# Rows of the second batch scaled in place, and their low halves subtracted on GpSimd

## The chip, the cores and the metric

The kernel runs on one core of a Trainium2 chip. The metric is the device time of one execution in microseconds (us): the median of three runs. A core has five engines with a queue of their own each, and each works through its queue in order: TensorE (PE, with its weight loads as PEld), VectorE (DVE), ScalarE (ACT), GpSimd (POOL), and SyncE (SP), which here only issues transfers.

## What is computed

Three layers one after the other, on 2304 rows (4 batches of 576) of 512 columns:

```python
def phi(x):                                   # q and k scaled by D**-0.25, D = 64
    proj = np.einsum('bhsd,md->bhsm', x, omega)
    sq = np.sum(x * x, axis=-1, keepdims=True) / 2.0
    h = proj - sq
    h = h - np.max(h, axis=-1, keepdims=True)
    return np.exp(h) / np.sqrt(m)
...
kv, z = np.einsum('bhsm,bhsd->bhmd', k_p, v), np.sum(k_p, axis=2)
num = np.einsum('bhsm,bhmd->bhsd', q_p, kv)
den = np.einsum('bhsm,bhm->bhs', q_p, z)[..., None] + 1e-06
attn = num / den                              # (4, 8, 576, 64), then rows of 512
h = attn @ w_in                               # 512 -> 2048
x = (h * (1 / (1 + np.exp(-1.702 * h)))) @ w_out
out = ((x @ w_a) * (x @ w_b)) @ w_out2        # 512 -> 1536 -> 512
```

## The kernel before, in words

Attention goes batch by batch, and in a batch by pairs of heads (hp 0 to 3), first k, then q. A pair is one tile `raw` of 128 partitions by T = 9 row groups by D = 64 columns, 576 columns in float32, loaded by SyncE. `features` makes the exponential features of a tile. For the first batch (`nm[1] == "0"`) TensorE does this in float32. For the others each number is split into a pair of float16 numbers, high and low half, in the tile `x16` (tag A, two buffers): line 402 writes the high half on ScalarE, scaled by S_QK = 32, line 403 the low half on VectorE, as the scaled row minus the high half. A transposing transfer (line 408, issued by SyncE) brings the pairs into `xt` (tag B, two buffers), and TensorE multiplies them with omega's two halves (lines 414 and 415). Beside that come the squares of the rows. For the second batch (SQACC = "1") ScalarE does them in nine pieces of 64 columns with an accumulating output (line 422), four before and five after the next load is issued; they overwrite the raw tile. Then row maxima (line 480, VectorE), the exponent's offset (line 486), the exponentials (line 446, ScalarE).

From the second batch on, attention is interleaved with the feed-forward layer of the batch before (`ffn1`): products `ph` (lines 654 to 656), a tanh (line 662, ScalarE), a product with it (line 665, VectorE), a float16 pair (lines 671 and 672), products `y` (lines 685 to 687). While the first batch's feed-forward layer runs, the weights `w_in` and `w_out` are loaded 1 MB at a time into two buffers and turned into float16 pairs: three passes on VectorE that put the float64 bits together as float32 (lines 214, 254 and 262), the high half on ScalarE (line 272), the low half on VectorE (line 221).

The order of each engine's instructions is made by a scheduler when the program is built, from the order of the code and from which buffers are free. An instruction that stands early in a queue and waits holds all that stands behind it. TensorE's filler products (line 1110, `idle`) stand between the first batch's last steps.

Of the kernel before, what the change touches and what calls it, by code (L numbers as in the profile page):

```python
# [12 lines left out]
AF = mybir.ActivationFunctionType  # L13
ALU = mybir.AluOpType
# [6 lines left out]
S_QK = 2.0**5  # L21
# [12 lines left out]
def fused_kernel(  # L34
# [13 lines left out]
    nc = tc.nc  # L48
# [17 lines left out]
    SQROOT = (0.5 / float(D) ** 0.5) ** 0.5  # L66
# [305 lines left out]
    def features(pool, nm, x, e16, e32, psp, extra, shift=0):  # L372
# [26 lines left out]
                nc.tensor.matmul(pvs[2][:, 0, :], xm[D:, :], om_f[D:], start=True, stop=True)  # L399
        else:  # L400
            x16 = pool.tile([P, T, 2, D], F16, tag="A", name=f"x16_{nm}")
            nc.scalar.activation(out=x16[:, :, 0, :], in_=x, func=AF.Copy, scale=S_QK)
            nc.vector.scalar_tensor_tensor(
                out=x16[:, :, 1, :], in0=x, scalar=S_QK, in1=x16[:, :, 0, :],
                op0=ALU.mult, op1=ALU.subtract,
            )
            xt = pool.tile([P, T, P], F16, tag="B", name=f"xt_{nm}")
            own["xt", nm] = nc.sync.dma_start_transpose(
                out=xt, in_=x16.rearrange("p t j d -> p (t j d)")
# [7 lines left out]
        groups, pairs = (GROUPS_F, PAIRS_F) if nm[1] == "0" else (GROUPS, PAIRS)  # L417
        sq = pool.tile([P, T], F32, tag="sq", name=f"sq_{nm}")

        def squares(lo, hi):  # L420
            for t in range(lo, hi):
                nc.scalar.activation(
                    out=x[:, t], in_=x[:, t], func=AF.Square, scale=SQROOT, accum_out=sq[:, t : t + 1]
                )

        if nm[1] in SQACC:
            yield
            squares(0, NT)
        else:
            nc.scalar.activation(out=x, in_=x, func=AF.Square, scale=SQROOT)  # L430
            yield
            nc.vector.tensor_reduce(out=sq, in_=x, axis=AX.X, op=ALU.add)
        extra()
        yield
        if nm[1] in SQACC:
            squares(NT, T)
# [27 lines left out]
        for gi in range(len(GROUPS) + 2):  # L464
# [4 lines left out]
            if 1 <= gi <= len(GROUPS):  # L469
# [4 lines left out]
                if pair[0] not in mxs:  # L474
# [6 lines left out]
                    out=mx[:, ms], in_=pv[:, : len(g), :], axis=AX.X, op=ALU.max  # L481
                )
                if gi - 1 == pair[-1]:

                    for o, i0, scale in ((mh, mx, PROJ), (nb, mh, -1.0)):
                        own["nb"] = nc.vector.scalar_tensor_tensor(
                            out=o[:, : z - a], in0=i0[:, : z - a], scalar=scale, in1=sq[:, a:z],
                            op0=ALU.mult, op1=ALU.subtract,
# [19 lines left out]
    def kphase32(pool, b, hp, psp, nxt, f32=True):  # L508
# [4 lines left out]
        if not f32:  # L513
# [20 lines left out]
            return  # L534
        e32 = pool.tile([P, T, M], F32, tag="e16", name=f"e32_{nm}")
        yield from features(pool, nm, raw, None, e32, psp, nxt)
        pk = psp()[:, 0 : 2 * VC].rearrange("p (h c) -> p h c", h=2)
        nc.tensor.matmul(pk, e32[:, 2 * NT, :], vm, start=True, stop=False)
# [8 lines left out]
    def qphase(pool, b, hp, xT, psp, nxt, f32=False):  # L547
# [5 lines left out]
        if f32:  # L553
            e32 = pool.tile([P, T, M], F32, tag="e16", name=f"e32_{nm}")
            yield from features(pool, nm, raw, None, e32, psp, nxt)
            eq = pool.tile([P, T * P], F32, tag="eqT", name=f"eT32_{nm}")
            eT = eq.rearrange("p (t m) -> p t m", m=P)
# [694 lines left out]
```

## Time and profile before

| | before |
|---|---|
| runs, us | 900.38, 901.43, 902.91 |
| median, us | 901.43 |
| the profiled execution, us | 899.4 |
| its span, first to last instruction, us | 897.6 |
| TensorE, VectorE, ScalarE, GpSimd busy, us | 872.3, 690.9, 455.3, 1.4 |
| 55 to 140 us: TensorE, VectorE, ScalarE busy, us | 81.81, 80.34, 61.58 |
| TensorE's granted clock in both stretches read below | 1.00 of full speed |

The profile is one execution. Its durations are of single instructions; where instructions of an engine overlap a little, the time from one start to the next is what counts. The second batch's attention lies between about 55 and 140 us; its first k tiles are begun some 20 us earlier, beside the first batch's last steps.

### The profile page before, as it was taken

How to read it: one execution, taken by the hardware profiler on the slowest of the kernel's cores; microseconds unless marked ns; L12 is line 12 of the kernel's file. 1: busy time of each engine (PE TensorE's matmuls, PEld its weight loads, DVE VectorE, ACT ScalarE, POOL GpSimd, SP SyncE). 2: the span in 40 equal slices, each digit the busy share in tenths (PEclk: the TensorE clock that was granted, in tenths of full speed). 3: DMA queues.
4: the chain of work that ended last, by engine and by line, in shares of the span. 5: the costliest groups of instructions: out<-in, count | busy, mean ns of one | idle time of the engine just before them, and what ended most of it. 6: DMA issues, size and time to landing. Idle time of an engine off the chain costs nothing.

```text
span 897.6 us, 17390 instructions
## 1 busy us (share of the span) xinstructions
PE 872.3 (97%) x7094; PEld 626.3 (70%) x7094; DVE 690.9 (77%) x1244; ACT 455.3 (51%) x1087; POOL 1.4 (0%) x10
## 2 busy tenths in 40 slices
PE   8999999999999999999999999999999999999997
PEld 6864555644554455444448888888888888888886
DVE  5889999778797787999923399777999558566766
ACT  7777774677566776454323354544443122233221
POOL 0000000000000000000000000000000000000000
PEclk9999999999999999999999999999999999999999
DMA  7856895453674323885401055212332022223312
GB/s 205 242 142 162 205 228 197 120 120 82 137 161 110 75 40 67 146 259 222 135 7 49 24 177 175 106 43 83 134 126 83 5 40 84 83 99 125 87 39 71
DMA packets 129343, 105.35 MB, mean 117 GB/s; under 512 B 97776, under 2 KB 111088, under 8 KB 127216
## 3 DMA queue, kind: packets, MB, share of 16 engines
q1 hardware_dynamic: 128558, 103.66, 41.2%
q8 instruction: 55, 0.90, 0.4%
q10 hardware_dynamic: 706, 0.59, 0.2%
q14 instruction: 24, 0.20, 0.1%
HBM read 71.07 MB, written 17.69 MB: 99 GB/s over the span
## 4 chain that ended last, share of the span: by engine, by line
PE 59%; DVE 21%; DMA 7%; ACT 7%; issue 2%; ACTq 0%; SPq 0%; DVEq 0%
PE ph L655 3%; PE ph L654 3%; PE ph L656 3%; PE y L685 3%; PE y L686 3%; PE y L687 3%; DMA xt_k<-x_k 3%; PE oA L904 2%; PE oA L902 2%; PE oA L903 2%; PE pbA L811 2%; PE pbA L809 2%; PE pbA L810 2%; PE paA L809 2%; PE pa L568 2%
## 5 line engine op out<-in xcount | busy, mean ns | idle before, releaser
L686 PE MATMUL y<-gl,w_out 128*128 128x512 f16 (+1 forms) x320 | 114.4, 358 | 0.9 <-DVE gl L672 0.8
L687 PE MATMUL y<-gh,w_out 128*128 128x512 f16 (+1 forms) x320 | 114.2, 358 | 0.0
L685 PE MATMUL y<-gh,w_out 128*128 128x512 f16 (+1 forms) x320 | 111.9, 358 | 0.8 <-ACT gh L671 0.7
L654 PE MATMUL ph<-xT,w_in 128*128 128x512 f16 x256 | 97.1, 379 | 1.5 <-DMA xT<-x_q_3x 0.7
L655 PE MATMUL ph<-xT,w_in 128*128 128x512 f16 x256 | 97.1, 379 | 0.3 <-DVE xT L623 0.3
L656 PE MATMUL ph<-xT,w_in 128*128 128x512 f16 x256 | 97.1, 379 | 0.0
L665 DVE SCALAR_TENSOR_TENSOR th<-th,ph 128x512 f32<-128x512 f32 (+1 forms) x80 | 50.3, 629 | 39.9 <-ACT th L662 39.7
L662 ACT ACTIVATE th<-ph 128x512 f32<-128x512 f32 (+1 forms) x80 | 44.2, 553 | 48.8 <-PE ph L656 48.8
L671 ACT ACTIVATE gh<-th 128x512 f16<-128x512 f32 (+1 forms) x80 | 47.1, 588 | 42.0 <-DVE th L665 41.9
L672 DVE SCALAR_TENSOR_TENSOR gl<-th,gh 128x512 f16<-128x512 f32 (+1 forms) x80 | 50.7, 634 | 15.9 <-ACT gh L671 15.5
L809 PE MATMUL paA<-forms,w_a 128*128 128x256 f16 (+1 forms) x240 | 61.0, 262 | 1.6 <-DVE ca L828 0.8
L809 PE MATMUL pbA<-forms,w_b 128*128 128x256 f16 (+1 forms) x240 | 61.1, 262 | 0.9 <-DVE cb L828 0.9
L811 PE MATMUL pbA<-forms,w_b 128*128 128x256 f16 (+1 forms) x240 | 61.0, 262 | 0.0
L811 PE MATMUL paA<-forms,w_a 128*128 128x256 f16 (+1 forms) x240 | 61.0, 262 | 0.0
L810 PE MATMUL pbA<-forms,w_b 128*128 128x256 f16 (+1 forms) x240 | 61.0, 262 | 0.0
L810 PE MATMUL paA<-forms,w_a 128*128 128x256 f16 (+1 forms) x240 | 61.0, 262 | 0.0
L902 PE MATMUL oA<-w_o,ab 128*128 128x256 f16 x216 | 58.9, 273 | 1.6 <-ACT ab L860 0.9
L904 PE MATMUL oA<-w_o,ab 128*128 128x256 f16 x216 | 58.9, 273 | 0.6 <-DVE ab L861 0.5
L903 PE MATMUL oA<-w_o,ab 128*128 128x256 f16 x216 | 58.9, 273 | 0.0
L817 ACT COPY ka<-paA 128x512 f32<-128x512 f32 (+1 forms) x30 | 16.3, 543 | 78.2 <-PE paA L811 78.1
L910 DVE SCALAR_TENSOR_TENSOR o<-oA,o 128x512 f32<-128x512 f32 (+1 forms) x45 | 28.5, 633 | 34.2 <-PE oA L904 34.2
L687 PEld LDWEIGHTS <-w_out 128*128 128x128 f16 x320 | 31.4, 98 | 29.9 <-issue 3.0
(209 smaller groups left out, 2353.5 us busy)
## 6 DMA issues: line engine op xcount, KB each, us to landing
wraw<-in_moe_w_out_dram SPq DMA_DIRECT2D x14, 1024.0 KB
forms<-fd SPq DMA_DIRECT2D x8, 1792.0 KB
wraw<-in_moe_w_in_dram SPq DMA_DIRECT2D x8, 1024.0 KB
fd<-forms SPq DMA_DIRECT2D x4, 1792.0 KB
wraw<-in_moe_w_a_dram SPq DMA_DIRECT2D x6, 1024.0 KB
wraw<-in_moe_w_b_dram SPq DMA_DIRECT2D x6, 1024.0 KB
vt<-in_v_dram SPq DMA_DIRECT2D x16, 256.0 KB
rawq<-in_q_dram SPq DMA_DIRECT2D x16, 256.0 KB
```

Of the source, the lines that this page charges most:

```text
L654: nc.tensor.matmul(ph[:, :n], w[:, 0, c, fs], xh(c), start=(c == 0), stop=False)
L655: nc.tensor.matmul(ph[:, :n], w[:, 0, c, fs], xl(c), start=False, stop=False)
L656: nc.tensor.matmul(ph[:, :n], w[:, 1, c, fs], xh(c), start=False, stop=(c == KC - 1))
L685: nc.tensor.matmul(o, w[:, 0, f % 4, cs], gh[f][:, :n], start=(f == 0), stop=False)
L686: nc.tensor.matmul(o, w[:, 0, f % 4, cs], gl[f][:, :n], start=False, stop=False)
L687: nc.tensor.matmul(o, w[:, 1, f % 4, cs], gh[f][:, :n], start=False, stop=(f == FC1 - 1))
L809: nc.tensor.matmul(o[:, i], wh, xh, start=first, stop=False, skip_group_check=True)
L810: nc.tensor.matmul(o[:, i], wh, xl, start=False, stop=False, skip_group_check=True)
L811: nc.tensor.matmul(o[:, i], wl, xh, start=False, stop=final, skip_group_check=True)
L902: nc.tensor.matmul(bank[:, t], lh, wh, start=first, stop=False, skip_group_check=True)
L903: nc.tensor.matmul(bank[:, t], lh, wl, start=False, stop=False, skip_group_check=True)
L904: nc.tensor.matmul(bank[:, t], ll, wh, start=False, stop=final, skip_group_check=True)
```

## The change

For the second batch alone, ScalarE first scales the raw tile in place (float32), then copies it to the high half; the low half is a plain difference of the two on GpSimd. The squares read the scaled rows, so their factor is divided by S_QK. All other batches stay as they were.

```diff
             x16 = pool.tile([P, T, 2, D], F16, tag="A", name=f"x16_{nm}")
-            nc.scalar.activation(out=x16[:, :, 0, :], in_=x, func=AF.Copy, scale=S_QK)
-            nc.vector.scalar_tensor_tensor(
-                out=x16[:, :, 1, :], in0=x, scalar=S_QK, in1=x16[:, :, 0, :],
-                op0=ALU.mult, op1=ALU.subtract,
-            )
+            if nm[1] == "1":
+                nc.scalar.activation(out=x, in_=x, func=AF.Copy, scale=S_QK)
+                nc.scalar.copy(x16[:, :, 0, :], x)
+                nc.gpsimd.tensor_tensor(
+                    out=x16[:, :, 1, :], in0=x, in1=x16[:, :, 0, :], op=ALU.subtract
+                )
+            else:
+                nc.scalar.activation(out=x16[:, :, 0, :], in_=x, func=AF.Copy, scale=S_QK)
+                nc.vector.scalar_tensor_tensor(
+                    out=x16[:, :, 1, :], in0=x, scalar=S_QK, in1=x16[:, :, 0, :],
+                    op0=ALU.mult, op1=ALU.subtract,
+                )
...
+        root = SQROOT / S_QK if nm[1] == "1" else SQROOT
...
-                    out=x[:, t], in_=x[:, t], func=AF.Square, scale=SQROOT, accum_out=sq[:, t : t + 1]
+                    out=x[:, t], in_=x[:, t], func=AF.Square, scale=root, accum_out=sq[:, t : t + 1]
```

The scheduler builds another order from it on all engines, in the second batch and, to a lesser degree, in the third. Lines behind the edit are 7 to 9 numbers higher in the changed kernel. In the rows below the names are the tiles written and read: `rawk_0_814` and `rawk_1_817` are the second batch's k tiles, `rawq_0_1102` (after: 1106) and so on its q tiles, `x_k_0` a tile of pairs, `eT_q_0` the first batch's transposed features.

ScalarE, at the end of the first batch's attention. Before:

```order
L446 ACTIVATE e_q_0_311<-pa,nb_q_0_1_425 128x128 x8
L544 COPY kv_128<-pa 128x130 [waits PE_49]
L430 ACTIVATE rawq_3_456<-rawq_3_456 128x576 [waits DMAHW6_49,DMAHW5_49,PE_49]
L402 ACTIVATE x_k_0_856<-rawk_0_814 128x9x64 [waits DMAHW2_49,DMAHW1_49,PE_49]
L563 COPY eT_q_0_514<-pa 128x512 [waits PE_49]
```

ScalarE, the same place in the changed kernel:

```order
L455 ACTIVATE e_q_0_311<-pa,nb_q_0_1_425 128x128 x8
L403 ACTIVATE rawk_1_817<-rawk_1_817 128x576 [waits DMAHW4_49,DMAHW3_49]
L553 COPY kv_128<-pa 128x130 [waits PE_49]
L403 ACTIVATE rawq_0_1106<-rawq_0_1106 128x576 [waits DMAHW6_49,DMAHW5_49]
L439 ACTIVATE rawq_3_456<-rawq_3_456 128x576 [waits PE_49]
L403 ACTIVATE rawq_1_1214<-rawq_1_1214 128x576 [waits DMAHW7_49,DMAHW0_49]
L403 ACTIVATE rawq_2_1329<-rawq_2_1329 128x576 [waits DMAHW2_49,DMAHW1_49,Activation_49]
L404 CAST x_k_0_856<-rawk_0_814 128x9x64 [waits PE_49,Activation_49]
L572 COPY eT_q_0_514<-pa 128x512 [waits PE_49]
```

Four in-place passes stand here that were not there (a fifth, of `rawk_0_814`, stands four rows above), those of the q tiles behind waits for their loads; the copy `eT_q_0` stands behind all of them.

ScalarE, around the first tanh of the feed-forward layer (`th_0`). Before:

```order
L622 CAST xT_100<-pa 128x512 [waits PE_49]
L272 ACTIVATE w_in_87<-wf_841 128x4x256 [waits DVE_49]
L662 ACTIVATE th_0_914<-ph_0_844 128x512 [waits PE_49]
L422 ACTIVATE rawk_1_817,sq_k_1_910<-rawk_1_817 128x64 [waits DVE_49]
L422 ACTIVATE rawk_1_817,sq_k_1_910<-rawk_1_817 128x64 x3
L662 ACTIVATE th_1_939<-ph_1_862 128x512 [waits PE_49]
```

ScalarE, the same place in the changed kernel:

```order
L631 CAST xT_100<-pa 128x512 [waits PE_49]
L431 ACTIVATE rawk_1_817,sq_k_1_912<-rawk_1_817 128x64
L404 CAST x_k_2_974<-rawk_2_820 128x9x64 [waits DMAHW5_49,Activation_49]
L403 ACTIVATE rawk_3_823<-rawk_3_823 128x576 [waits DMAHW1_49,DMAHW0_49]
L403 ACTIVATE rawq_3_1444<-rawq_3_1444 128x576 [waits DMAHW7_49]
L404 CAST x_k_3_1065<-rawk_3_823 128x9x64 [waits DMAHW2_49,Activation_49]
L272 ACTIVATE w_out_89<-wf_882 128x1024 [waits DVE_49]
L671 ACTIVATE th_0_916<-ph_0_844 128x512 [waits PE_49]
L671 ACTIVATE th_1_941<-ph_1_863 128x512 [waits PE_49]
```

The casts of the third and fourth k tiles and two in-place passes now stand ahead of the first tanh. The cast of the fourth waits (DMAHW2) for the transposing transfer of the second, whose buffer of pairs it takes.

## Rows read from the trace of the kernel before

**Rows 1.** The page: busy us of each engine (share of the span), number of instructions.

```profile
PE 872.3 (97%) x7094; PEld 626.3 (70%) x7094; DVE 690.9 (77%) x1244; ACT 455.3 (51%) x1087; POOL 1.4 (0%) x10
```

**Rows 2.** Busy time in two stretches; stretch, its length, engines, granted clock, DMA share, GB/s.

```profile
55.00:140.00 85.00, 81.81 (x509) 45.12 (x507) 80.34 (x134) 61.58 (x239) 0.00 (x0) 1.00 0.76 201
28.00:55.00 27.00, 26.93 (x236) 24.04 (x235) 22.85 (x56) 22.33 (x76) 0.00 (x0) 1.00 0.72 187
```

**Rows 3.** Waits of TensorE, 55 to 160 us: total us, times, longest.

```profile
PE pa L414 <- ACT e_k L446: 1.7, 1, 1.7
PE pa L414 <- ACT e_q L446: 0.7, 1, 0.7
PE ph L654 <- DVE th L665: 0.4, 1, 0.4
PE ph L655 <- DVE xT L623: 0.3, 1, 0.3
```

**Rows 4.** Groups on VectorE, 55 to 140 us: busy us, mean ns | idle before, releaser.

```profile
L254 DVE SCALAR_TENSOR_TENSOR wf<-wraw,wf 128x1024 int32<-128x1024 int32 x11 | 13.4, 1221 | 0.0
L262 DVE SCALAR_TENSOR_TENSOR wf<-wraw,wf 128x1024 int32<-128x1024 int32 x11 | 13.4, 1218 | 0.0
...
L672 DVE SCALAR_TENSOR_TENSOR gl<-th,gh 128x512 f16<-128x512 f32 x12 | 8.1, 685 | 0.0
...
L221 DVE SCALAR_TENSOR_TENSOR w_in<-wf,w_in 128x1024 f16<-128x1024 f32 x6 | 7.3, 1218 | 0.3 <-ACT w_in L272 0.3
L221 DVE SCALAR_TENSOR_TENSOR w_out<-wf,w_out 128x1024 f16<-128x1024 f32 x6 | 7.3, 1212 | 0.0
...
L403 DVE SCALAR_TENSOR_TENSOR x_q<-rawq,x_q 128x576 f16<-128x576 f32 x4 | 3.0, 754 | 1.3 <-ACT x_q L402 1.3
L403 DVE SCALAR_TENSOR_TENSOR x_k<-rawk,x_k 128x576 f16<-128x576 f32 x3 | 2.2, 749 | 0.0
```

**Rows 5.** Chain of waits, 59 to 90 us: start us, us, what.

```profile
62.80 0.67 DVE x_k L403
...
72.81 3.23 DMA xt_k<-x_k
...
76.12 0.68 ACT x_q L402
...
78.82 0.22 PE pa L414
...
83.25 6.76 DMA xt_k<-x_k
```

**Rows 6.** ScalarE in order of time, 27.9 to 35.6 us: start, us, [idle before, releaser].

```profile
27.95 0.37 ACT L446 ACTIVATE e_q<-pa,nb_q 128x128 f32<-128x128 f32 x1 [0.60 <-DVE nb_q L486]
...
31.91 0.27 ACT L544 COPY kv<-pa 128x130 f32<-128x130 f32 x1 [0.81 <-PE pa L540]
32.47 0.68 ACT L430 ACTIVATE rawq<-rawq 128x576 f32<-128x576 f32 x1 [0.28 <-PE pa L384]
33.78 0.68 ACT L402 ACTIVATE x_k<-rawk 128x576 f16<-128x576 f32 x1 [0.63 <-PE pa L399]
34.37 0.58 ACT L563 COPY eT_q<-pa 128x512 f32<-128x512 f32 x1
...
35.37 0.27 ACT L563 COPY eT_q<-pa 128x128 f32<-128x128 f32 x1
```

**Rows 7.** TensorE in order of time: product reading eT_q, first feed-forward product.

```profile
36.45 1.33 PE L568 MATMUL pa<-kv,eT_q 128*128 128x65 f32 x10
...
54.63 0.38 PE L654 MATMUL ph<-xT,w_in 128*128 128x512 f16 x1
```

**Rows 8.** Groups on GpSimd, whole span: its longest instruction.

```profile
L313 POOL MEMSET vm<- 128x520 f32 x1 | 0.5, 531 | 0.0
```

**Rows 9.** ScalarE in order of time, 60 to 64 us.

```profile
61.64 0.60 ACT L662 ACTIVATE th<-ph 128x512 f32<-128x512 f32 x1 [1.48 <-PE ph L656]
63.50 0.26 ACT L422 ACTIVATE rawk<-rawk 128x64 f32<-128x64 f32 x1 [1.26 <-DVE x_k L403]
```

## The prediction, made before the changed kernel ran

> **What bounds the kernel now.** I read the busy shares first, then the stretch that the change touches, then its waits and its chain. TensorE is busy for 97% of the span and GpSimd for 1.4 us [rows 1]; over the whole program nothing but TensorE's own work is long enough to set the time. The second batch's attention runs in one stretch, from about 55 to 140 us, under the first batch's feed-forward tile, and there the page's average misleads. In those 85 us TensorE is busy for 81.81, VectorE for 80.34 and ScalarE for 61.58 [rows 2]. So two engines are close to full there, and VectorE is the one that the change relieves. In the stretch ahead of it (28 to 55 us, the first batch's last steps) TensorE is busy for 26.93 of 27 us, partly with filler products, and ScalarE for 22.33 [rows 2].
>
> What TensorE waits for in the stretch is little: the four waits of [rows 3] sum to 3.1 us, and two smaller ones of 0.2 us each are left out there. Two name VectorE (0.4 and 0.3 us), two name ScalarE's exponentials (1.7 and 0.7 us). The chain says how they came about. Shortly before the 0.4 us wait, VectorE itself stands on the chain, with one of this change's subtractions (0.67 us) [rows 5]. Before the 1.7 us wait a transposing transfer holds ScalarE, which waits for it in front of its scaling of a q tile and only then comes to the exponentials that TensorE needs [rows 5]. These waits are all that the change can win here: 3.1 us, or 3.5 with the small ones, of some 900.
>
> **What it takes off VectorE.** Eight subtractions at line 403 go, one for each pair of heads of k and q in the second batch. Each takes about 0.75 us by itself and 0.67 us of VectorE's time from its start to the next one's [rows 4, 5]. Seven lie in the stretch (four for q, three for k [rows 4]), one before it: 7 x 0.67 = 4.7 us. VectorE also stands idle for 1.3 us ahead of two of the q ones, because they wait for ScalarE [rows 4]; that goes too. Together 6.0 of VectorE's 85 us.
>
> **What it adds to ScalarE.** Eight more passes over 576 columns. One scaled pass of that size takes 0.68 us, and 0.59 us from its start (33.78) to the next start (34.37) [rows 6]: 8 x 0.59 = 4.7 us in all. ScalarE is 73% busy in the stretch, so what matters is where they stand. The in-place pass needs only the loaded rows and no free buffer of float16 pairs, so five of the eight move ahead, into the end of the first batch, in front of the copy eT_q that starts at 34.37. ScalarE has idle pieces there of 0.60, 0.81, 0.28 and 0.63 us [rows 6]. Two passes fit into the first two. Three do not fit wholly: 3 x 0.59 - 0.28 - 0.63 = 0.86 us late. The product that reads eT_q starts at 36.45 [rows 7], while its last copy starts at 35.37 and takes 0.27 [rows 6], so it has 36.45 - 35.64 = 0.81 us to spare. What is left is about 0.1 us. One unknown remains: ScalarE waits in order for the third q tile's load. If that lands late, the exponentials, eT_q and a weight conversion queued behind it wait as well. The trace does not show its landing, so I bound it: nothing, or 1 us. I take 0.2 us for this place, nearer to nothing because the loads were issued several microseconds earlier.
>
> The other place is the end of the first batch's rows, about 55 to 64 us. There the squares of the second k tile now wait for GpSimd, and the last copy into xT stands behind them on ScalarE; four passes and the casts of two k tiles stand ahead of the first tanh. ScalarE idles 1.48 and 1.26 us between 60 and 64 us [rows 9], which covers four passes of 0.59 us (2.4 us). What the waits add on top I put between 0 and 2 us, and take 0.5.
>
> **What it gives GpSimd.** Eight subtractions of 576 columns with two operands read from SBUF. GpSimd has no such row in the trace. The nearest is a fill of 520 columns, 0.53 us [rows 8], or 0.59 us for 576 columns. That is the lower end; three such passes, one for each operand and one for the result, are 1.8 us, the upper end. I take two passes, 1.2 us. Its own duration is mostly hidden. The transposing transfers that wait for it are also paced by TensorE giving back their target buffers. What is not hidden is whether GpSimd and VectorE can read SBUF at once. If they can, nothing is added. If GpSimd keeps VectorE out for as long as it runs, seven pieces of 1.2 us (8.4 us) come on top, more than the 6.0 that went. No row shows it, since GpSimd never worked beside VectorE here. I take the middle, 4.2 us, as one of the two ends alone would need a reason.
>
> What VectorE does there makes this the main question: 13.4 + 13.4 + 7.3 + 7.3 + 8.1 = 49.5 of its 80.3 us are instructions with two operands in SBUF, without those that go [rows 4]. On this the Trainium skill speaks against the change: in SBUF — State Buffer, section Who interferes with whom, it says that a VectorE instruction with two SBUF inputs and a GpSimd instruction that reads SBUF exclude each other, and that the one that comes second stands still until the first is through. By that rule this term is the whole 8.4 us and not 4.2, and the time comes out as the second rival below; no run here shows it yet. The price of the subtraction by the GPSIMD Engine Reference, section Performance versus the Vector engine (2.6 cycles for an element at 1.2 GHz), is an estimate of 1.25 us, which would leave the sum as it is.
>
> **The sum.** VectorE: -4.7 - 1.3 + 4.2 = -1.8 us in the stretch. The two waits of TensorE that name VectorE hold 0.7 us [rows 3], and TensorE is nearly full beside it, so I let 0.3 us of it arrive at the end. With the two places on ScalarE: +0.2 + 0.5 - 0.3 = +0.4 us. The profiled execution took 899.4 us (897.6 us span and 1.8 us around it), the median of the three runs is 901.43, so +2.0 us over the profile; I put the change on the median: 901.43 + 0.4 = 901.8 us.
>
> **The rivals.**
> *No interference (faster).* GpSimd and VectorE run side by side, all 6.0 us are won, and the six waits of TensorE (3.1 + 0.4 = 3.5 us) close nearly all: -3.3 us, with +0.2 at the start: 898.3 us. For it: VectorE stands directly before a wait of TensorE in the chain [rows 5], and earlier subtractions let the k transfers go earlier. Against it: the largest wait hangs on a transfer and on ScalarE's order [rows 5], and ScalarE gets more to do.
>
> *GpSimd holds VectorE up (slower).* Each GpSimd subtraction that lies in the stretch stops VectorE. VectorE was busy for 80.34 us and idle for 4.66, 1.3 of which goes [rows 2, 4]. It needs 80.34 - 4.7 + 3.36 = 79.0 us without GpSimd's pieces; with seven of 1.2 us 87.4, with seven of 1.8 us 91.6, against 85. Converted weights, tanh products and row maxima then come 2.4 to 6.6 us later, and TensorE, which has only some 3 us of idle time, waits for them. With 1.5 us each it is +4.5, and +0.7 from ScalarE: 906.6 us (904.5 to 908.7). It decides from 6.0 / 7 = 0.86 us of standstill for each subtraction. For it: two thirds of VectorE's time there are two-operand instructions. It is the case in which the change does not do what it says: the work would leave VectorE and its time would not. It is also the case of the Trainium skill's rule on the shared port named above.
>
> *ScalarE's order (slower, a little).* The cast of the fourth k tile now stands ahead of the first tanh and waits until the second k tile's transfer has freed a buffer. In this kernel one such transfer took 3.23 us to release ScalarE, a later one 6.76 [rows 5]. If the one in question is of the second kind, that is 3.5 us more; the squares and casts that stand between cover a part, and I let 2.0 us reach the tanh and the products behind it: 901.4 + 0.7 + 2.0 = 904.1 us.
>
> **How the numbers follow.** I give the forecast 0.45, no interference 0.20, the hold-up 0.25, ScalarE's order 0.10. The predicted time is 901.8 us. From 898.0 to 907.0 it holds the forecast (900.5 to 903.5), the fast case, ScalarE's order and two thirds of the hold-up: about 0.85. A measurement tells some 0.3%, or 2.7 us, from no change, so faster means under 898.7 and slower over 904.1. Faster: most of the first rival, 0.18. Slower: nearly all of the hold-up, half of ScalarE's order and a tail of the forecast, 0.32. The same: 0.50.
>
> **What would show it.** In the changed kernel's profile: GpSimd's eight subtractions and their length (0.6 to 1.8 us, 1.2 by my price); VectorE's two-operand instructions in 55 to 140 us, whose mean of 1.22 us for 1024 columns stays as it is where nothing holds them and grows, or whose starts spread, where GpSimd does; the start of the first feed-forward product, 54.63 now [rows 7], which I expect at most 0.5 us later; TensorE's waits in 55 to 160 us, 3.5 us now, which I expect between 2.5 and 4.5. I am wrong if the start moves by more than 1 us, if VectorE loses more than 6 us to GpSimd, or if a wait for GpSimd itself stands on the chain.

## The result, and the profile after

The changed kernel takes 905.97 us, the median of 7 runs from 904.74 to 912.2, beside 902.79 for the kernel before (7 runs, 900.38 to 903.83). The ratio is 1.0055, with a 95% interval of 1.0028 to 1.0081. Measured again beside the experiments below it was 1.0100 (1.0072 to 1.0128). By the two ratios the change costs 5 and 9 us (2.5 to 11.5 with the intervals). Two executions near 1510 us, at a granted clock of about 0.55, are left out of every median and ratio below. The profiled execution took 904.89 us, its span 903.0, and 5.4 us more than the span before.

First the busy line of the page after, to set beside [rows 1].

```profile
PE 872.0 (97%) x7094; PEld 627.0 (69%) x7094; DVE 693.7 (77%) x1236; ACT 459.7 (51%) x1095; POOL 16.1 (2%) x18
```

VectorE lost eight instructions (1244 to 1236) and is busy for 2.8 us longer. The two stretches of [rows 2], after (stretch, length, busy time of each engine, granted clock, DMA share, GB/s):

```profile
28.00:55.00 27.00, 25.53 (x224) 22.64 (x222) 23.18 (x51) 23.71 (x74) 2.16 (x1) 1.00 0.73 190
55.00:140.00 85.00, 78.85 (x499) 44.69 (x498) 82.53 (x127) 65.08 (x249) 12.56 (x7) 1.00 0.71 196
```

TensorE is busy for 1.40 us less in the first and 2.96 us less in the second. From 200 to 300 us it is 1.1 us less (97.46 before, 96.38 after), in code that the change doesn't touch. These three make the 5.4 us of the span, nearly. VectorE in the second stretch has 4.7 us of subtractions less and is busy for 2.2 us more: 80.34 before, 82.53 after.

TensorE's waits from 55 to 160 us, as [rows 3] (total us, times, longest):

```profile
PE pa L421 <- ACT e_k L455: 2.3, 3, 1.2
PE ph L663 <- DVE th L674: 2.2, 1, 2.2
PE ph L664 <- DVE xT L632: 1.2, 1, 1.2
PE pa L421 <- ACT e_q L455: 0.3, 1, 0.3
```

Together 6.0 us in place of 3.5. The wait for th went from 0.4 to 2.2, the one for xT from 0.3 to 1.2.

**Where GpSimd meets VectorE.** GpSimd's subtractions in two groups (busy us, mean ns), and then three of the eight in order of time (start, us):

```profile
L405 POOL TENSOR_TENSOR x_k<-rawk,x_k 128x576 f16<-128x576 f32 x4 | 7.7, 1914 | 57.3 <-DVE mx_q L489 34.3 <-ACT x_k L404 23.0
L405 POOL TENSOR_TENSOR x_q<-rawq,x_q 128x576 f16<-128x576 f32 x4 | 7.1, 1765 | 42.6 <-ACT x_q L404 42.6
```

```profile
56.62 2.32 POOL L405 TENSOR_TENSOR x_k<-rawk,x_k 128x576 f16<-128x576 f32 x1 [18.12 <-ACT x_k L404]
...
76.97 2.22 POOL L405 TENSOR_TENSOR x_q<-rawq,x_q 128x576 f16<-128x576 f32 x1 [10.00 <-ACT x_q L404]
...
103.75 1.28 POOL L405 TENSOR_TENSOR x_q<-rawq,x_q 128x576 f16<-128x576 f32 x1 [11.14 <-ACT x_q L404]
```

And VectorE beside them:

```profile
57.71 1.37 DVE L638 TENSOR_TENSOR x16r<-xf_q,x16r 64x128 f16<-64x128 f32 x1
...
76.70 0.16 DVE L495 SCALAR_TENSOR_TENSOR mh_k<-mx_k,sq_k 128x5 f32<-128x5 f32 x1
76.83 1.23 DVE L254 SCALAR_TENSOR_TENSOR wf<-wraw,wf 128x1024 int32<-128x1024 int32 x1
77.97 1.24 DVE L495 SCALAR_TENSOR_TENSOR nb_k<-mh_k,sq_k 128x5 f32<-128x5 f32 x1
...
103.33 0.68 DVE L489 TENSOR_REDUCE mx_k<-pa 128x4 f32<-128x512 f32 x1
103.94 2.17 DVE L254 SCALAR_TENSOR_TENSOR wf<-wraw,wf 128x1024 int32<-128x1024 int32 x1
```

Read them together. At 76.97 GpSimd starts while VectorE is inside a two-operand instruction (line 254, until 78.06). It comes through only behind that and ends at 79.19: 2.22 us. VectorE's next two-operand instruction, five columns that take 0.16 us elsewhere, starts at 77.97 and ends at 79.21. At 103.75 VectorE reads PSUM (line 489); GpSimd runs at once, and 1.28 us is its own length. VectorE's next instruction (line 254) takes 2.17 in place of 1.22. Seven instructions in the stretch (one of them line 214, with one operand) are lengthened so, by 1.09, 0.47, 0.45, 1.08, 0.96, 0.95 and 1.08 us: 6.1 us.

One of them can be followed to TensorE. The five columns at 77.97 are the offset that the exponentials e_k need, and ScalarE stands for them:

```profile
79.24 0.26 ACT L431 ACTIVATE rawk<-rawk 128x64 f32<-128x64 f32 x1 [1.39 <-DVE nb_k L495]
```

It comes to e_k at 80.22, and TensorE, which waits for e_k, stands 1.18 us until 81.38. By these rows 1.08 us of it are GpSimd's hold-up.

**Where the start moved.** ScalarE in order of time ([rows 6] before), and TensorE's first product behind the copy eT_q:

```profile
33.32 0.74 ACT L403 ACTIVATE rawq<-rawq 128x576 f32<-128x576 f32 x1
34.95 0.68 ACT L403 ACTIVATE rawq<-rawq 128x576 f32<-128x576 f32 x1 [0.89 <-DMA rawq<-in_q_dram]
...
36.10 0.58 ACT L572 COPY eT_q<-pa 128x512 f32<-128x512 f32 x1
```

```profile
36.73 0.33 PE L570 MATMUL pa<-ident,e_q 128*128 128x128 f32 x1 [1.29 <-ACT eT_q L572]
```

ScalarE waits 0.89 us for the third q tile's load, and the copy eT_q starts at 36.10 and not at 34.37. The one that waits for it is not the product of [rows 7] but a transposition (line 570) that needs the PSUM buffer which eT_q empties. The first feed-forward product starts at 56.23 and not at 54.63.

### The profile page after: what moved, and what is told of

The parts are those of the page before. It is cut to its first block, busy times and chain, and to the rows that moved or that the text cites. A ratio compares the mean times of both kernels' runs of the same rounds, so it can differ in the third digit from the quotient of the medians.

```text
span 903.0 us, 17404 instructions
## 1 busy us (share of the span) xinstructions
PE 872.0 (97%) x7094; PEld 627.0 (69%) x7094; DVE 693.7 (77%) x1236; ACT 459.7 (51%) x1095; POOL 16.1 (2%) x18
## 4 chain that ended last, share of the span: by engine, by line
PE 58%; DVE 24%; ACT 7%; DMA 7%; issue 3%; SPq 0%; ACTq 0%; DVEq 0%
PE y L694 3%; PE ph L663 3%; PE ph L664 3%; PE y L695 3%; PE ph L665 3%; PE y L696 3%; PE oA L913 2%; PE oA L911 2%; PE oA L912 2%; PE pa L577 2%; PE pbA L818 2%; PE pbA L820 2%; PE pbA L819 2%; DVE wf L254 2%; PE paA L818 2%
## 5 line engine op out<-in xcount | busy, mean ns | idle before, releaser
L826 ACT COPY ka<-paA 128x512 f32<-128x512 f32 (+1 forms) x30 | 16.3, 544 | 78.2 <-PE paA L820 78.1
L664 PEld LDWEIGHTS <-w_in 128*128 128x128 f16 x320 | 31.4, 98 | 30.8 <-issue 3.9
```

The costliest lines, as they stand in the source:

```text
L664: nc.tensor.matmul(ph[:, :n], w[:, 0, c, fs], xl(c), start=False, stop=False)
```

## The experiments

Each is given as a ratio to the kernel before on the same chip, with its interval. The first group takes the change apart.

| kernel | median us (before) | ratio, 95% interval |
|---|---|---|
| changed, first | 905.97 (902.79) | 1.0055 (1.0028 to 1.0081) |
| changed_again | 907.7 (900.25) | 1.0100 (1.0072 to 1.0128) |
| sub_on_vector | 908.7 (900.17) | 1.0097 (1.0075 to 1.012) |
| q_passes_held | 905.57 (900.17) | 1.0059 (1.0043 to 1.0074) |
| held_on_vector | 901.31 (900.17) | 1.0012 (1.0001 to 1.0023) |
| unscaled_on_gpsimd | 903.75 (900.17) | 1.0048 (1.0029 to 1.0068) |
| unscaled_on_vector | 900.64 (900.25) | 1.0005 (0.9994 to 1.0015) |

**ScalarE's passes alone.** Theory A: GpSimd holds VectorE up. Theory B, its rival: ScalarE's extra passes and where they stand. First the subtraction back on VectorE, then q's passes held back, then both.

```diff
-                nc.gpsimd.tensor_tensor(
+                nc.vector.tensor_tensor(
                     out=x16[:, :, 1, :], in0=x, in1=x16[:, :, 0, :], op=ALU.subtract
```

> The changed kernel with one thing undone: the eight subtractions of the second batch go back to VectorE (as a plain subtraction of the scaled rows), the in-place scaling stays on ScalarE. Theory A, GpSimd holds VectorE up: the start stays late (first feed-forward product at about 56.2 us, as in the changed kernel), VectorE's 64x128 product at 57.7 us falls back from 1.37 to 0.27 us and the 128x5 one from 1.24 to 0.16, TensorE's waits in 55 to 165 us fall from 6.0 to about 3.5 to 4.5, and the time is 1.5 to 2.5 us over the kernel before (ratio 1.002 to 1.003). Theory B, ScalarE's eight extra passes and their places do it all: start at 56.2, waits still near 6, time as the changed kernel's, 1.005 of the kernel before.

```diff
-                nc.scalar.activation(out=x, in_=x, func=AF.Copy, scale=S_QK)
+                if nm[0] == "q":
+                    with tc.issue_after(own["eT"]):        # the last eT_q copy
+                        nc.scalar.activation(out=x, in_=x, func=AF.Copy, scale=S_QK)
+                else:
+                    nc.scalar.activation(out=x, in_=x, func=AF.Copy, scale=S_QK)
```

> The changed kernel with the four in-place passes over q held back on ScalarE until the last eT_q copy of the first batch; the subtractions stay on GpSimd. If the late start comes from the three q passes that stand ahead of eT_q and from the wait for a q load among them, the first feed-forward product is back at 54.6 to 54.9 us (56.23 in the changed kernel). Theory A (GpSimd): the waits behind it stay, so the time is 1.5 to 4 us over the kernel before (1.002 to 1.004). Theory B (ScalarE's order): the time is within 1 us of the kernel before (1.000 to 1.001).

> Both of the former: q passes held back and the subtractions on VectorE; what is left of the change is eight passes on ScalarE. Theory A: start at 54.6 to 54.9, no lengthened VectorE products, time within 1 us of the kernel before. Theory B: with the passes still on ScalarE the exponentials and the first tanh in 55 to 80 us come late and 1 to 2 us of the 5 remain, 904 to 905.

With the subtraction back on VectorE nothing was won; it is 8.7 us over the kernel before. ScalarE's order shows a part of why (start, us, idle before):

```profile
62.12 0.68 ACT L403 ACTIVATE rawk<-rawk 128x576 f32<-128x576 f32 x1 [0.59 <-DMA rawk<-in_k_dram]
...
62.90 0.58 ACT L631 CAST xT<-pa 128x512 f16<-128x512 f32 x1
```

An in-place pass waits for a load a second time, now that of the fourth k tile, in front of the last copy into xT; the wait for th is 2.2 us here too. Holding the four q passes back changes this order, and it takes 7.6 of the 8.7 us away (1.0097 to 1.0012). In q_passes_held the first feed-forward product is back:

```profile
54.58 0.38 PE L668 MATMUL ph<-xT,w_in 128*128 128x512 f16 x1
```

In held_on_vector it starts at 57.05 us, but everything is later there: the first product of the first batch's k with v starts at 19.03 us and not at 16.66, and from one to the other it is 38.0 us in both kernels. Yet with GpSimd subtracting and the passes held it is still 1.0059. So eight passes on ScalarE cost about 1 us where they stand well. Their early places cost 7.6 us where VectorE subtracts; where GpSimd does, between nothing and 4 us (1.0055 and 1.0100 against 1.0059). Both theories hold a part: B was right on the start (39.3 us behind that product in sub_on_vector, 39.6 in the changed kernel) and wrong on q_passes_held, A was wrong on sub_on_vector.

**GpSimd alone.** Without scaling there is no in-place pass; the factor 32 goes into the scales behind the products.

```diff
-                nc.scalar.activation(out=x, in_=x, func=AF.Copy, scale=S_QK)
                 nc.scalar.copy(x16[:, :, 0, :], x)
...
-                    bias=nb[:, i - a : i - a + 1], scale=PROJ,
+                    bias=nb[:, i - a : i - a + 1], scale=PROJ * S_QK if nm[1] == "1" else PROJ,
```

> GpSimd alone: the second batch's rows are not scaled at all (pairs of the unscaled rows, the factor 32 is put into the scales of the maxima and the exponentials), so ScalarE has as many passes as in the kernel before and GpSimd does the eight subtractions. Theory A: start at 54.6 to 55, VectorE's instructions that start while GpSimd runs are lengthened by 0.5 to 1.1 us, TensorE's waits in 55 to 165 us are 4 to 6 us, time 1 to 4 us over the kernel before. Theory B: without the extra passes nothing is late, and VectorE's relief counts: the time is that of the kernel before or up to 3 us less (0.997 to 1.000).

> The unscaled kernel with the subtractions on VectorE, as a control: no more work on any engine than in the kernel before, and the order of the third batch is the one of the kernel before. Both theories: within 1 us of the kernel before (0.999 to 1.001); if the unscaled form itself cost something, it would show here.

GpSimd's share is the difference, some 4 us (1.0048 against 1.0005). The start is at 54.32 us, the waits in 55 to 160 us sum to 5.8. VectorE from 55 to 140 us, on GpSimd's kernel and then with the subtractions on VectorE:

```profile
55.00:140.00 85.00, 79.15 (x498) 44.62 (x497) 81.93 (x126) 62.48 (x236) 12.00 (x7) 1.00 0.75 205
```

```profile
55.00:140.00 85.00, 82.21 (x506) 45.41 (x506) 80.08 (x134) 62.81 (x244) 0.00 (x0) 0.98 0.77 197
```

VectorE is busy for 81.93 us without the subtractions and for 80.08 with them: its relief has gone, and more.

> The changed kernel as it is, beside the pieces of the change on the same chip: the two runs of its parts (1.0097 with the subtractions on VectorE, 1.0059 with the q passes held) stand on both sides of its own 1.0055, which was measured beside other runs. Both theories: 1.004 to 1.007 (904 to 907 us beside about 900.3).

It came out at 1.0100, above the 1.007 expected at most. Two of its six runs were at 913.6 us with a granted clock of 0.988 and 0.990 over the span (see the last section). Over its six runs the granted clock was 0.9947 on the mean, and 0.9989 over those of the kernel before beside them; by an estimate from these, 0.0042 x 908 = 3.8 us of its 9 are the clock. The parts do not add up: about 1 us for the passes, 4 for GpSimd and 7.6 for the early places of the q passes would be some 12.6, and the change costs 5 to 9. With the early places, moving the subtraction from VectorE to GpSimd costs nothing (1.0097 against 1.0055 and 1.0100); without them it costs 4 us (1.0012 against 1.0059, 1.0005 against 1.0048).

**Exclusion, measured by itself.** The kernel before, with a train on GpSimd that nobody waits for, started behind the second k tile's high half. It ran from 43.5 to 110 us, the fills from 44.4 to 95.

```diff
+            if nm == "k1_1":
+                sp = own["spare"]
+                nc.gpsimd.tensor_copy(sp[:, :, 0:D], x16[:, 0:2, 0, :])
+                for _ in range(50):        # train_fill: 130 times nc.gpsimd.memset(sp, 0.5)
+                    nc.gpsimd.tensor_tensor(
+                        out=sp, in0=own["ident"][:, None, :].to_broadcast([P, 2, P]),
+                        in1=om_h[:, None, :].to_broadcast([P, 2, P]), op=ALU.subtract,
+                    )
```

> The kernel before, unchanged, with 50 more subtractions on GpSimd in a row (256 columns, two operands from SBUF, result into a spare tile) from about 56 us on; nobody waits for them. Theory A, GpSimd and VectorE exclude each other where both read two operands: in the train's stretch VectorE's two-operand instructions (1.22 us for 1024 columns at lines 254 and 262) grow by a part of a piece or more (0.3 to 1 us), GpSimd's pieces are uneven, one-operand ones (0.69 us at line 214) and those that read PSUM stay; the time grows by several us. If they share nothing: VectorE's lengths as before within 0.05 us, time within 1 us of the kernel before.

> The same train with 130 fills of the same spare tile (256 columns, nothing read) in place of the subtractions. If it is the reading of operands that excludes VectorE: VectorE's lengths as in the kernel before, time within 1 us of it. If any GpSimd instruction beside VectorE does it: as with the subtractions.

The subtractions cost 9.2 us (909.56 beside 900.4; 1.0101, 1.0086 to 1.0115), the fills nothing (900.46; 1.0001, 0.9990 to 1.0012). VectorE's groups beside the subtractions, 57 to 110 us (busy us, mean ns | idle):

```profile
L254 DVE SCALAR_TENSOR_TENSOR wf<-wraw,wf 128x1024 int32<-128x1024 int32 x6 | 7.9, 1321 | 0.0
L214 DVE TENSOR_SCALAR wf<-wraw 128x1024 int32<-128x1024 int32 x6 | 5.0, 836 | 0.0
L488 DVE TENSOR_REDUCE mx_k<-pa 128x4 f32<-128x512 f32 x7 | 4.7, 676 | 0.0
...
L494 DVE SCALAR_TENSOR_TENSOR nb_k<-mh_k,sq_k 128x5 f32<-128x5 f32 x3 | 1.9, 629 | 0.0
```

and beside the fills:

```profile
L254 DVE SCALAR_TENSOR_TENSOR wf<-wraw,wf 128x1024 int32<-128x1024 int32 x7 | 8.5, 1218 | 0.0
...
L214 DVE TENSOR_SCALAR wf<-wraw 128x1024 int32<-128x1024 int32 x7 | 5.0, 719 | 0.3 <-DMA wraw<-in_moe_w_out_dram 0.3
```

Five columns take 629 ns and not 160, and 1024 columns 1321 and not 1218, as means over those that met a piece and those that did not. In the changed kernel, where single meetings can be read, the wait is about the same for a short instruction (1.08 us) and a long one (0.95). The row maxima, which read PSUM, stay at 676. It is the reading, not GpSimd's being busy. (The expectation had line 214, one operand, unaffected; it grew.) This is the rule of the Trainium skill, SBUF — State Buffer, section Who interferes with whom, that the prediction weighed; the traces agree with it, the fills included, which it exempts as instructions that only write.

The 9.2 us are not all standstill. TensorE came to wait 8.0 us between 55 and 160 us (2.9 with the fills), and its clock fell (length, busy times, then the granted clock):

```profile
80.00:85.00 5.00, 3.85 (x21) 2.33 (x21) 5.00 (x8) 2.47 (x14) 4.69 (x5) 0.52 0.03 10
```

Over its four runs the granted clock was 0.9962 on the mean, beside 0.9986 for the kernel before; by an estimate from these, 0.0024 x 910 = 2.2 us of the 9.2 are the clock.

**Which pieces.** Only q's, only k's, or each cut in three.

```diff
+                low = nc.gpsimd if nm[0] == "q" else nc.vector        # unscaled_k_gpsimd: "k"
+                low.tensor_tensor(out=x16[:, :, 1, :], in0=x, in1=x16[:, :, 0, :], op=ALU.subtract)
...
+                for ts in (slice(0, 3), slice(3, 6), slice(6, 9)):    # unscaled_thirds
+                    nc.gpsimd.tensor_tensor(
+                        out=x16[:, ts, 1, :], in0=x[:, ts], in1=x16[:, ts, 0, :], op=ALU.subtract
+                    )
```

> The unscaled kernel with only the four q subtractions on GpSimd, k's on VectorE. Theory A, each piece makes VectorE stand for about 0.9 us wherever it falls: half of the loss of the unscaled kernel, 1.3 to 2.2 us over the kernel before. Theory E, the place decides: what hurts is the hold in front of the first feed-forward products, where k's pieces fall (56 to 67 us); q's pieces fall where VectorE has some room, 0 to 0.8 us over the kernel before.

> The same with only the four k subtractions on GpSimd, q's on VectorE. Theory A: 1.3 to 2.2 us over the kernel before. Theory E: 2.5 to 4.5 us over it, with the wait of about 2 us for th at 67 to 70 us, as when all eight are on GpSimd.

> The unscaled kernel with each GpSimd subtraction cut into three pieces of 192 columns. If the length of one hold-up matters (a VectorE instruction of 0.16 us in TensorE's path stands for a whole piece), holds of 0.3 to 0.5 us in place of 0.9 to 1.1 bring the time to 1 to 2.5 us over the kernel before. If it is the sum of the holds, nothing is gained: VectorE stands for as long or longer (24 pieces), 3 to 5 us over it.

q's alone cost 2.6 us (902.87; 1.0033, 1.0021 to 1.0045). k's alone cost nothing (900.91; 1.0001, 0.9991 to 1.0010). In thirds it is worse, 906.53 (1.0063, 1.0046 to 1.0079). So it is neither a fixed price for each piece nor k's place at the head of the stretch; theory E had the sides exchanged. Why thirds lose more I did not follow. TensorE's waits from 55 to 160 us with k's alone:

```profile
PE ph L661 <- DVE th L672: 2.3, 1, 2.3
...
PE pa L419 <- ACT e_k L453: 0.2, 1, 0.2
```

and with q's alone:

```profile
PE pa L419 <- ACT e_k L453: 3.4, 3, 1.7
PE ph L661 <- DVE th L672: 0.4, 1, 0.4
```

k's subtractions let the k transfers go earlier (the second tile's is issued at 57.1 us and not at 63.5), so the old wait for e_k of 1.7 us goes, and a new one for th of 2.3 comes. q's leave the old wait and add a second of 1.4. Their first piece also shows the other side of the exclusion:

```profile
77.33 4.05 POOL L405 TENSOR_TENSOR x_q<-rawq,x_q 128x576 f16<-128x576 f32 x1 [75.34 <-ACT x_q L403]
```

It starts while VectorE is inside line 254 (until 77.97 us); lines 221 and 262, which VectorE starts at 77.89 and 79.02, go ahead of it at their full speed (1.22 us each), and it ends at 81.38. The rule as the prediction puts it, that the one that comes second stands still until the first is through, does not hold of this piece: by its end GpSimd came through only behind the third instruction, though spans on GpSimd are rough in the profile.

The second wait is another matter. In front of the cast of a q tile (88.52 us) ScalarE stands 3.89 us for a transposing transfer, and only behind the cast come the exponentials that TensorE needs at 91.23. In unscaled_on_vector the cast stands behind these exponentials. TensorE's second wait for e_k in the changed kernel (0.95 us, until 92.78) has the same form:

```profile
90.07 0.67 ACT L404 CAST x_q<-rawq 128x576 f16<-128x576 f32 x1 [1.68 <-DMA xt_k<-x_k]
91.61 1.37 ACT L455 ACTIVATE e_k<-pa,nb_k 128x128 f32<-128x128 f32 x5
```

In the kernel before these exponentials start at 86.42, ahead of the cast (90.04). So this is ScalarE's order and a transfer, and not VectorE's standstill. Whether it makes all that q's pieces cost is not shown.

**Orders that moved.** The kernels with k's subtractions on GpSimd have a wait of 1.5 to 3.5 us for th, and another order on several queues; the one with q's alone has 0.4. sub_on_vector has it too (2.2 us), where GpSimd subtracts nothing. I undid orders of SyncE, of the third batch and of ScalarE, one by one.

On SyncE, the second k tile's transfer stands ahead of a weight load, and waits for GpSimd (theory C):

```diff
+            with tc.issue_after(loads[{"k1_0": -1, "k1_1": -2}.get(nm, 0)]):    # weight loads so far
+                own["xt", nm] = nc.sync.dma_start_transpose(...)
```

> The unscaled kernel with GpSimd's eight subtractions, and the transposing transfers of the first two k tiles held in SyncE's order behind the weight loads that stood ahead of them in the kernel before. Theory C, the weight load late behind a transfer that waits for GpSimd: the load is issued at 59 us and not at 60.4, VectorE's weight shift after it is not late, TensorE's one wait of 1.9 to 2.2 us for th at 67 to 70 us falls to 0.5 us or less, and of the 3.6 to 4.3 us over the kernel before 1.5 to 2.5 go. Theory A, VectorE held up by GpSimd directly: that wait stays over 1.5 us and the time stays 3 to 4 us over the kernel before.

> The changed kernel with both orders mended: q passes held back on ScalarE behind the last eT_q copy, and the weight loads ahead of the first two k transfers in SyncE's order; GpSimd keeps its subtractions. Theory C: 1 to 2.5 us over the kernel before (1.001 to 1.003). Theory A: 4 to 5.5 us over it, as with the q passes held alone (1.0059 there).

The load went out 2.6 us earlier (55.84 and not 58.49 us). The wait for th only fell from 1.9 to 1.5, and the times did not fall: 906.37 (1.0057, 1.0038 to 1.0077) and 906.55 (1.0062, 1.0044 to 1.0081). Theory C falls.

In the third batch, VectorE's order of weight sums and low halves changed, and several of GpSimd's kernels wait 1.2 to 3.1 us for eqT_q near 270 us (theory D). later_order gives the kernel before this order; the two others give it back.

```diff
+                if behind is not None and n == 1:        # later_order, in the weight sums
+                    with tc.issue_after(behind):         # the last low half of e_q, tile q2_3
+                        nc.vector.tensor_tensor(out=sx[:, o], in0=x, in1=y, op=op)
```

> The kernel before with one order in the third batch (near 260 us) made as the changed kernel has it: on VectorE the last three weight sums (sx) of one weight chunk stand behind the low halves of the last q tile's exponentials (e_q) and not ahead of the first of them; nothing of the second batch is touched. Theory D, the change costs time far behind its place, by another order there: SyncE issues this tile's transposing transfer about 1.8 us after a weight load and not 2.6 us after it, the issue takes 4 to 5 us and not 3.3, TensorE waits 1.3 to 3.3 us for eqT_q near 267 us where it waits for nothing now, and the time is 1.5 to 4 us over the kernel before (1.002 to 1.004). Theory A, all of the loss is made in the second batch by GpSimd and ScalarE: within 1 us of the kernel before.

> The changed kernel with that one order in the third batch put back (two of the sums ahead of the e_q low half). Theory D: TensorE's wait for eqT_q near 270 us falls from 1.5 us to 0.3 or less, and of the 5 us over the kernel before 1.5 to 3 go (1.002 to 1.004). Theory A: 1.0055 as the changed kernel.

> The unscaled kernel with GpSimd's subtractions and that order put back: what is left of the change is GpSimd's exclusion of VectorE in the second batch. Theory D: 0 to 1.5 us over the kernel before (the offset at 142 us was 0.2 us in the unscaled kernel). Theory A: 3.5 to 4.5 us over it, as the unscaled kernel (1.0048).

later_order takes as long as the kernel before: 900.46, 1.0005 (0.9994 to 1.0016), with a wait of 0.3 us there. Giving the order back left waits of 1.2 and 1.1 us; the times are 907.58 (1.0088, 1.0070 to 1.0106) and 902.93 (1.0030, 1.0018 to 1.0042). Theory D falls: that wait varies with nothing changed at its place (1.0 us in unscaled_on_vector, none in the kernel before; 3.1 in sub_on_vector), and I don't know what sets it.

On ScalarE, the fourth k tile's cast and a weight conversion stand ahead of the first tanh (theory F, the prediction's third rival). Before and after, the first tanh starts at 61.64 and 66.83 us. In the changed kernel the cast waits for nothing; it is VectorE for which ScalarE waits, behind it:

```profile
64.34 0.66 ACT L404 CAST x_k<-rawk 128x576 f16<-128x576 f32 x1
65.86 1.06 ACT L272 ACTIVATE w_out<-wf 128x1024 f16<-128x1024 f32 x1 [0.87 <-DVE wf L262]
66.83 1.55 ACT L671 ACTIVATE th<-ph 128x512 f32<-128x512 f32 x3
```

In unscaled_on_gpsimd the cast waits for a transfer as the rival has it:

```profile
62.17 0.67 ACT L403 CAST x_k<-rawk 128x576 f16<-128x576 f32 x1 [1.24 <-DMA xt_k<-x_k]
63.49 1.06 ACT L272 ACTIVATE w_out<-wf 128x1024 f16<-128x1024 f32 x1 [0.65 <-DVE wf L262]
64.54 1.89 ACT L670 ACTIVATE th<-ph 128x512 f32<-128x512 f32 x3
```

```diff
+                if nm == "k1_3":
+                    with tc.issue_after(own["th"]):        # behind the third tanh
+                        nc.scalar.copy(x16[:, :, 0, :], x)
...
+                tc.add_manual_dep(own["conv"], own["th"].name, ...)    # w_out behind the second
```

> The unscaled kernel with GpSimd's eight subtractions and ScalarE's order of the kernel before around the first tanh: the cast of the fourth k tile behind the third tanh, the weight conversion (w_out) behind the second one; in the unscaled kernel both stand ahead of the first, and the cast waits 1.24 us there for a transposing transfer. Theory F, the third rival of the prediction (ScalarE's order) is half of what GpSimd's version loses: the first tanh is at 61.5 to 62.5 us and not at 64.5, TensorE's wait for th at 67.7 us falls from 1.9 us to 0.6 or less, and the time is 1 to 2.5 us over the kernel before (1.001 to 1.003) and not 4.3 (1.0048). Theory A, it is all the exclusion: the wait stays over 1.5 us in one place or another, and the time at 3.5 to 4.5 us over the kernel before.

> The changed kernel with every ScalarE order mended that moved: q's in-place passes and the fourth k tile's two passes behind the first tanhs, the weight conversion behind the second. GpSimd keeps its eight subtractions, so the exclusion stays. Theory F: start at 54.6 us, the wait for th 0.6 us or less, 2 to 4 us over the kernel before (1.002 to 1.004), against 1.0055 and 1.0100 of the changed kernel. Theory A: 5 us or more (1.0059 as with the q passes held alone).

Neither won: 906.0 (1.0073, 1.0055 to 1.0091) and 906.11 (1.0064, 1.0052 to 1.0076), with waits for th of 1.9 us. The first tanh did not come earlier. In unscaled_tanh_first it starts at 65.31 us (65.11 in changed_orders_mended), and it is TensorE for which ScalarE waits there:

```profile
65.31 1.24 ACT L674 ACTIVATE th<-ph 128x512 f32<-128x512 f32 x2 [3.61 <-PE ph L668]
```

By the records TensorE starts 30 products of ph ahead of this tanh in both kernels, and 23 in the kernel before: its order had moved too. VectorE in unscaled_tanh_first, in order of time:

```profile
65.39 0.69 DVE L214 TENSOR_SCALAR wf<-wraw 128x1024 int32<-128x1024 int32 x1 [1.18 <-DMA wraw<-in_moe_w_in_dram]
66.01 0.68 DVE L492 TENSOR_REDUCE mx_k<-pa 128x4 f32<-128x512 f32 x1
66.61 1.21 DVE L254 SCALAR_TENSOR_TENSOR wf<-wraw,wf 128x1024 int32<-128x1024 int32 x1
67.74 1.27 DVE L683 SCALAR_TENSOR_TENSOR th<-th,ph 128x512 f32<-128x512 f32 x2
```

VectorE waits 1.18 us for a late weight load, and three of its instructions (two weight passes and row maxima) now stand between line 262 and its first th. In the kernel before, th came straight behind line 262:

```profile
63.38 1.22 DVE L262 SCALAR_TENSOR_TENSOR wf<-wraw,wf 128x1024 int32<-128x1024 int32 x1
64.52 0.68 DVE L665 SCALAR_TENSOR_TENSOR th<-th,ph 128x512 f32<-128x512 f32 x1
```

In sub_on_vector the same three stand there (from 67.25 us, th at 69.59). In held_on_vector they do not (th at 66.81), and TensorE does not wait for th. So this wait goes with the order and not with the exclusion. Its reasons lie in a row on SyncE, ScalarE, TensorE and VectorE, and taking one away shows the next. No run mended them together, and none mended VectorE's or TensorE's order, so that these make the wait is read from the traces and not tested. As the k kernel has this wait and costs nothing, it is not the whole loss either.

No version beat the kernel before.

## Why the prediction was wrong

It said 901.8 us and no measurable change; the changed kernel is slower. That it lies near the second rival (906.6) is luck. The rival's own sum takes 1.5 us for each piece; with the 0.87 us that were measured it gives 79.0 + 6.1 = 85.1 of 85 us, 0.1 us over, and so 901.4 + 0.1 + 0.7 = 902.2. The same holds of the forecast: with 6.1 in place of 4.2 VectorE's balance is +0.1 and not -1.8 us, which is far from 5 us. The step that failed is the one common to both: that what VectorE wins or loses over the 85 us decides, and that the moved orders add 0.2 us at the start and 0.5 at the tanh. In the profile, 1.6 us were lost at the start, 2.5 in TensorE's waits up to 160 us, and 1.1 from 200 to 300 us, for which the sum had no term.

**What it takes off VectorE** was right: 4.7 us of the stretch, gone from the rows.

**What it gives GpSimd** was mis-sized, in the step that took the middle of an open question. The standstill is whole: 6.1 us over seven pieces, 0.87 us each, where the sum had 4.2 of at most 8.4. That lies just above the 0.86 us from which the rival decides, and VectorE's load did not fall (82.53 us, 80.34 before). GpSimd's own piece is 1.28 us, as priced (1.2); its row is up to 2.32, over the upper end of 1.8, because waiting for VectorE is counted in it. The reason against the whole rule was only that no row of before showed it; the trains show it.

**The start** failed. The sum had +0.2 us and a bound of 1 us for the load; the start moved by 1.6. I had compared the delay with the slack of the product that reads eT_q. The transposition that needs the emptied PSUM buffer had almost none. The load's wait was within the bound (0.89). Held back, the q passes left the start where it was: 38.3 and 38.0 us behind the first product of k with v, 38.0 in the kernel before, 39.6 in the changed one.

**ScalarE's order** was priced at 0.5 us, with 2.0 for the third rival. A wait of 2.2 us for th came, but not as the rival told it: in the changed kernel the fourth k tile's cast did not wait for a transfer (it did in unscaled_on_gpsimd, 1.24 us). Putting ScalarE's order back did not remove the wait. Of the idle time that was to cover the four passes, the piece of 1.26 us lies behind the first tanh [rows 9]; only the 1.48 us lie ahead of it. What I had left out is VectorE's order, in which row maxima and two weight passes now stand ahead of the first th, and TensorE's. A stand of ScalarE for a transfer, the rival's mechanism, did reach TensorE at another place: the cast of a q tile (1.68 us), with a wait of 0.95 us behind it.

**The waits** in 55 to 160 us are 6.0 us, not 2.5 to 4.5. Of the rivals, no interference is excluded by the trains. Two of the three signs of being wrong came: the start moved by more than 1 us, and VectorE lost more than 6 us to GpSimd. The hold-up is confirmed as a mechanism: VectorE stands, and one of TensorE's waits (1.18 us) follows from it. GpSimd alone costs 2.7 to 4.3 us without the scaling (two kernels that differ in order, unscaled_load_first and unscaled_tanh_first, lost 5.1 and 6.6). How this splits between the standstill and the orders that moved with it stays open, since each order mended alone gave nothing back that is clear of noise.

## What to carry to other kernels

Before work goes from VectorE to GpSimd, count how much of VectorE's time beside it is instructions with two SBUF operands. Where it was most of it, as here, the relief came back as standstill (6.1 us for 4.7), and a five-column instruction stood as long as a large one. What that costs at the end is another question: four pieces cost nothing and four others 2.6 us, and the sum over VectorE did not tell which. Compare the order of every queue, TensorE's too, before and after. A step that needs only its input is pulled ahead by a scheduler and brings its wait for a load along: look for who needs what stands behind it, the buffer as well as the data, on every queue.

## What the runs showed of the chip that was not expected

A wait of TensorE can cost more than its length. In q_passes_held it stood 2.4 us for eqT_q until about 270 us. The stretches around it (length, busy times, then the granted clock ahead of the DMA share):

```profile
265.00:270.00 5.00, 2.57 (x24) 1.13 (x21) 3.31 (x10) 3.30 (x7) 0.00 (x0) 1.00 1.13 286
270.00:275.00 5.00, 5.00 (x42) 2.52 (x40) 4.49 (x12) 1.51 (x4) 0.00 (x0) 0.66 0.42 69
275.00:280.00 5.00, 5.00 (x25) 2.27 (x24) 4.20 (x7) 3.81 (x8) 0.00 (x0) 1.00 0.60 114
```

For a part of the middle one the granted clock was at its lower level, 1.2 and not 2.4 GHz; (1 - 0.66) x 5 = 1.7 us of full speed are lost behind a wait of 2.4. Over the 20 profiles (18 experiments and the two kernels) TensorE stood idle 19 times for 1.8 us or more between 28 and 420 us. In eight of these the clock fell during the wait or soon after it; behind the eleven others it did not. Two more falls came behind shorter waits (1.73 us in unscaled_on_vector, 1.40 and 0.93 in train_subtract). The profiled run of the changed kernel has none, though its wait is 2.2 us; in sub_on_vector one came behind the like wait (0.66 from 70 to 75 us). Its runs scatter more than those of the kernel before, and the slowest have the lowest clock (904.7 to 913.6 us at clocks of 1.000 to 0.988).

Two things far from the change varied also. The first product of the first batch's k with v started between 16.3 and 19.0 us. The three latest (18.2 to 19.0 us, in unscaled_thirds, sub_on_vector and held_on_vector) had a granted clock of 0.89 over the first 16 us, and 1.00 before; the rest I did not follow. And the wait for eqT_q near 270 us was anything from nothing to 3.1 us. Differences under 3 us were therefore read from the medians, not from one profile.
